# Seven products in one more tile, sums stored one after another, and separate PSUM banks at the end

## The chip, the cores and the metric

The kernel runs on one core of a Trainium2 chip. The metric is the device time of one execution in microseconds (us). The profile gives a second figure, the *span*, from the first to the last recorded event on the core; it is 1.7 to 3.2 us shorter than the device time. A profile also gives the mean granted clock of the matrix engine (1.00 is full speed).

Engines: PE multiplies matrices (PEld is its weight load, which overlaps), DVE is the vector engine, ACT the scalar engine, POOL the GpSimd engine, SP the engine that issues most stores. PSUM is the memory that PE writes its results into; it is divided into banks.

## The reference

Attention over 8 batches, 8 heads, 576 positions and head size 64, with a local mask for half of the heads and a strided one for the others, and then a gated product on the 4,608 tokens. Only the second part is touched:

```python
def _moe_ref(x, w_a, w_b, w_out):          # x: 4608 x 512
    a = x @ w_a                            # 512 x 1536
    b = x @ w_b
    return (a * b @ w_out).astype(np.float32)   # w_out: 1536 x 512
```

## The kernel before

The 4,608 tokens are 9 tiles of 512 (`TTOK`). For each tile the kernel makes 12 chunks (`FD`) of `pf = (x w_a) * (x w_b)`, 8 matmuls of 512 columns per chunk (the *projections*), and then the output `pf @ w_out`. The attention of later batches is woven between these matmuls. `do(slot, ...)` puts work after a given slot; there are 16 slots per tile, 12 for the projections and 4 for the output.

The output is computed in two ways. The ordinary way (`ffn_y`, in tiles 0 to 2) takes 48 matmuls of 512 columns. In the tiles of `FAST_Y` the rows, the contraction and the columns are each cut into two halves, and the four blocks of the output come from seven products of half size instead of eight. That takes 84 matmuls of 256 columns, but it needs sums of `pf` (`fast_s`, made by DVE for each tile, written into `ps`), sums of `w_out` (`fast_w`, made once, written into `wf`) and some additions and subtractions after the products.

```python
FAST_Y = (3, 4, 5, 6, 7, 8)
HT = TTOK // 2;  HN = d_model // 2;  FG = FD // 2

def fast_w(n, gs):                         # one of five sums of w_out, for the groups gs of 6
    a, b, op = (...)[n]
    nc.vector.tensor_tensor(wf[:, n, gs], a[:, gs], b[:, gs], op=op)

def fast_s(t, n, gs):                      # five sums of pf; group outermost: [group][sum, row]
    if t not in pss:
        pss[t] = nat.tile([128, 5 * FD * TTOK // 4], BF16, ...).rearrange("p (g m) -> p g m", g=FG)
    s = pss[t][:, gs]
    x = pfs[t].rearrange("p (g e) (i m) -> p g e i m", e=2, i=2)[:, gs]
    if n == 0:   tensor_tensor(s[:, :, 0:HT], x[:, :, 0, 0], x[:, :, 1, 1], op=ALU.add)
    elif n == 1: ...                       # sums 1 and 2 in one operation
    else:        ...                       # sums 3 and 4 in one operation

def products(t):                           # weights of a matmul: 128 neighbouring columns
    full = lambda e, i: (lambda g, q: pf[:, 2 * g + e, HT * i + 128 * q:HT * i + 128 * (q + 1)])
    summed = lambda n: (lambda g, q: s[:, g, HT * n + 128 * q:HT * n + 128 * (q + 1)])
    ...

def y_store(eng, t, y, i, q, n=...):       # 128 rows: 8 runs (a) of 16 rows (s)
    rows = out[...].rearrange("(q a i s) c -> a s i q c", q=2, i=2, s=16)
    eng.dma_start(out=rows[:, :, i, q], in_=y[i][:, q, n])
```

The last tile has its own form, `y_tail`, which runs the seven products once for each half `q` of the rows, to be done sooner:

```python
for q in range(2):
    if q == 0:
        bank = {x: mm_bank([128, HN]) for x in "abcd"}
    else:                                  # the last pass: two tiles of two banks each
        o = psum4["o"].tile([128, 2, 512], F32, tag="o", name="end")
        st = pst.tile([128, 2, 512], F32, tag="st", name="end")
        bank = {"a": o[:, 0, :HN], "b": o[:, 1, :HN], "c": st[:, 0, :HN], "d": st[:, 1, :HN]}
    for k in "3412567":
        ...                                # six matmuls, then ACT, DVE or POOL, then a store
```

The schedule of the parts that move: two fills of value buffers by POOL in slots 18 and 19 (tile 1), and ten pieces of the weights' sums by DVE in slots 33 to 42 (tile 2).

The softmax here doesn't subtract the row's maximum and nothing guards it: scores larger than these inputs give would overflow.

Of the kernel before, what the change touches and what calls it, by code (L numbers as in the profile page):

```python
# [7 lines left out]
F32 = mybir.dt.float32  # L8
BF16 = mybir.dt.bfloat16
# [17 lines left out]
FAST_Y = (3, 4, 5, 6, 7, 8)  # L27
# [3 lines left out]
def kernel(  # L31
# [10 lines left out]
    nc = tc.nc  # L42
# [122 lines left out]
    HT = TTOK // 2  # L165
    HN = d_model // 2
# [18 lines left out]
    def load_qk(b, strided, heads=range(HL), names="kq"):  # L185
        for nm in names:
            src = {"k": k, "q": q}[nm]
            if b < FIRST_D:
                n, R, h0 = (NP, RS, HL) if strided else (96, RL, 0)
                w0 = {"k6": 0, "q6": 1536, "k8": 3072, "q8": 5120}[f"{nm}{R}"]  # L190
                if b not in shared:
                    shared[b] = nat.tile([128, 5 * FD * TTOK // 4], BF16, tag="shared", name="shared")
# [304 lines left out]
    def step_X(b, c):  # L497
# [16 lines left out]
                 10.5: "V6", 11: "S0 Tk1", 11.5: "V7", 12: "Tq1 S1", 12.5: "V0 X2", 13: "S2", 13.5: "V1 X3 S3", 14: "V2",  # L514
# [5 lines left out]
    FN = {"Tk": step_Tk, "Tq": step_Tq, "S": step_S, "V": step_V, "X": step_X}  # L520
# [51 lines left out]
    def fast_s(t, n, gs):  # L572
        if t not in pss:
            pss[t] = nat.tile([128, 5 * FD * TTOK // 4], BF16, tag="shared", name="ps").rearrange("p (g m) -> p g m", g=FG)
        s = pss[t][:, gs]
        x = pfs[t].rearrange("p (g e) (i m) -> p g e i m", e=2, i=2)[:, gs]
        if n == 0:
            nc.vector.tensor_tensor(s[:, :, 0:HT], x[:, :, 0, 0], x[:, :, 1, 1], op=ALU.add)  # L578
        elif n == 1:
            nc.vector.tensor_tensor(s[:, :, HT:3 * HT].rearrange("p g (i m) -> p g i m", i=2), x[:, :, 0], x[:, :, 1], op=ALU.add)  # L580
        else:
            nc.vector.tensor_tensor(s[:, :, 3 * HT:].rearrange("p g (e m) -> p g e m", e=2), x[:, :, :, 1], x[:, :, :, 0],
                                    op=ALU.subtract)
# [3 lines left out]
    def products(t):  # L587
        pf, s = pfs[t], pss[t]
        full = lambda e, i: (lambda g, q: pf[:, 2 * g + e, HT * i + 128 * q:HT * i + 128 * (q + 1)])
        summed = lambda n: (lambda g, q: s[:, g, HT * n + 128 * q:HT * n + 128 * (q + 1)])  # L590
        wsum = lambda n: (lambda g: wf[:, n, g])
        wfull = lambda e, j: (lambda g: wov[:, e, j, g])
        return {"3": ("a", full(0, 0), wsum(0)), "4": ("b", full(1, 1), wsum(1)), "1": ("c", summed(0), wsum(2)),
                "2": ("b", summed(2), wfull(0, 0)), "5": ("a", summed(1), wfull(1, 1)), "6": ("c", summed(3), wsum(3)),
                "7": ("d", summed(4), wsum(4))}
# [7 lines left out]
    def y_store(eng, t, y, i, q, n=slice(0, d_model)):  # L603
        rows = out[TTOK * t:TTOK * (t + 1), n].rearrange("(q a i s) c -> a s i q c", q=2, i=2, s=16)
        eng.dma_start(out=rows[:, :, i, q], in_=y[i][:, q, n])
# [4 lines left out]
    def y_plan(t):  # L610
# [4 lines left out]
        def store_half(i):  # L615
            for q in range(2):
                y_store(nc.sync, t, y, i, q)
# [38 lines left out]
    def y_tail(t):  # L656
# [4 lines left out]
        for q in range(2):  # L661
            if q == 0:
                bank = {x: mm_bank([128, HN]) for x in "abcd"}
            else:
                o = psum4["o"].tile([128, 2, 512], F32, tag="o", name="end")
                st = pst.tile([128, 2, 512], F32, tag="st", name="end")
                bank = {"a": o[:, 0, :HN], "b": o[:, 1, :HN], "c": st[:, 0, :HN], "d": st[:, 1, :HN]}
# [74 lines left out]
    with tc.manual_schedule(engines={ENG.PE, ENG.SP, ENG.Pool, ENG.DVE, ENG.Activation}):  # L742
# [80 lines left out]
        def do(i, fn, *args):  # L823
            at.setdefault(i, []).append(lambda: fn(*args))
# [34 lines left out]
        do(18, fill_v, vl_buf[1])  # L859
        do(19, fill_v, vs_buf[1])  # L860
        for n in range(5):
            for z in range(2):
                do(33 + 2 * n + z, fast_w, n, slice(3 * z, 3 * z + 3))
# [48 lines left out]
```

## Time and profile before

| | |
|---|---|
| device time, median of 6 runs (the 3 given and 3 beside the changed kernel) | 337.37 us (336.41 to 339.04) |
| span of the profiled run | 335.3 us |
| tiles 0, 1, 2 | 41.19, 35.94, 35.21 us |
| tiles 3 to 7 | 34.23, 34.47, 34.22, 33.98, 29.89 us |
| projections of tile 8 | 20.72 us |
| its output, from the first product to the last DVE operation | 11.84 us |
| from that operation to the end of the span | 4.63 us |

A tile runs from its first projection to that of the next one. The prediction below shows the page, the chain and the waits. More views, two here and two behind the prediction:

The first is the timeline of the last pass of the last tile. Columns: start, length, engine, line, operation, out<-in, size, count, and in brackets the idle time before it and what ended that.

```profile
323.50 0.82 PE L678 MATMUL end<-wf,pf 128*128 128x256 bf16 x6
324.36 0.37 ACT L683 COPY ya<-end 128x256 f32<-128x256 f32 x1 [1.59 <-PE end L678]
...
324.78 0.82 PE L678 MATMUL end<-wf,pf 128*128 128x256 bf16 x6 [0.46 <-ACT ya L683]
...
327.46 0.81 PE L678 MATMUL end<-wo_sb,ps 128*128 128x256 bf16 x6 [0.46 <-ACT y_sb L693]
...
330.38 0.29 DVE L706 TENSOR_TENSOR y_sb<-ye,mm 128x128 f32<-128x128 f32 x1
```

PE stands still each time another engine reads the other half of the same two-bank tile. The last DVE operation ends at 330.67, 7.17 us after the pass began.

The second is DVE's timeline in tile 0, around the place where the change puts half of the weights' sums.

```profile
47.38 0.69 DVE L433 TENSOR_TENSOR xr<-o,rc 72x512 bf16<-72x512 f32 x1
51.54 0.46 DVE L374 TENSOR_TENSOR p<-p,mask_l 128x576 int16<-128x576 int16 x1 [3.47 <-ACT p L364]
```

DVE is idle for 3.47 us between these two.

The third is the busy time by stretch after the last DVE operation, when only stores are under way. Columns: stretch, length, busy PE, PEld, DVE, ACT, POOL with counts, clock, mean busy share of the 16 DMA engines, GB/s.

```profile
330.70:333.50 2.80, 0.00 (x0) 0.00 (x0) 0.00 (x0) 0.00 (x0) 0.00 (x0) 1.00 0.40 118
331.10:331.60 0.50, 0.00 (x0) 0.00 (x0) 0.00 (x0) 0.00 (x0) 0.00 (x0) 1.00 0.51 152
```

In no half microsecond after the last DVE operation is the share above 0.54: about eight of sixteen engines.

### The profile page before, as it was taken

The numbers are of one execution on the slowest core, as the hardware profiler recorded it, in microseconds if no ns is written. First come the engines' busy times: TensorE is split into PE (matmuls) and PEld (weight loads), VectorE is DVE, ScalarE is ACT, GpSimd is POOL, SyncE is SP. The second block draws the span as 40 slices with busy tenths as digits, with TensorE's granted clock in tenths as the row PEclk, the third lists the DMA queues.
The fourth block names the chain that finished last, engine by engine and source line by source line (L and its number), as shares of the span: only waits on it lengthen the run. The fifth ranks groups of instructions, "written<-read, shape, count | busy, mean of one in ns | idle before, by whom it ended". The sixth has DMA issues, their size and how long they took to land.

```text
span 335.3 us, 7662 instructions
## 1 busy us (share of the span) xinstructions
PE 326.2 (97%) x2814; PEld 201.8 (60%) x2814; DVE 254.7 (76%) x489; ACT 202.8 (60%) x329; POOL 173.4 (52%) x295
## 2 busy tenths in 40 slices
PE   8999999999999999999999999999999999999992
PEld 6654555455555555556999885568556844674472
DVE  5867566768878985799999999999877845738641
ACT  5663955468678865776587757875788533223320
POOL 8945836499956644765577457754312031312011
PEclk9999999999999999999999999999999999999999
DMA  9999999599999599969888998899123021003013
GB/s 155 148 203 196 201 181 188 120 191 70 131 221 155 86 99 158 129 116 92 69 83 139 179 98 75 142 164 107 25 62 119 2 73 54 1 12 116 0 29 98
DMA packets 102173, 37.60 MB, mean 112 GB/s; under 512 B 77432, under 2 KB 97784, under 8 KB 102136
## 3 DMA queue, kind: packets, MB, share of 16 engines
q0 software_dynamic: 87760, 19.58, 64.4%
q1 hardware_dynamic: 14104, 17.34, 17.7%
q8 instruction: 22, 0.36, 0.4%
q10 hardware_dynamic: 272, 0.20, 0.2%
q14 instruction: 15, 0.12, 0.1%
HBM read 39.71 MB, written 9.44 MB: 147 GB/s over the span
## 4 chain that ended last, share of the span: by engine, by line
PE 75%; DMA 12%; POOL 7%; DVE 2%; issue 2%; ACT 0%; DVEq 0%; POOLq 0%
PE mm L545 44%; PE mm L650 14%; PE mm L730 7%; DMA vl<-in_v_dram 4%; PE o L454 4%; PE st L356 3%; DMA shared<-in_k_dram 3%; DMA wa_sb<-in_moe_w_a_dram 3%; PE end L678 1%; PE mm L678 1%; POOL shared L195 1%; DMA kl<-in_k_dram 1%; POOL ql L210 1%; DMA natk<-in_k_dram 1%; POOL vl L222 1%
## 5 line engine op out<-in xcount | busy, mean ns | idle before, releaser
L545 PE MATMUL mm<-xT,wb_sb 128*128 128x512 bf16 (+1 forms) x472 | 110.2, 357 | 0.1
L545 PE MATMUL mm<-xT,wa_sb 128*128 128x512 bf16 (+1 forms) x472 | 110.3, 358 | 0.0
L562 ACT COPY a_sb<-mm 128x512 f32<-128x512 f32 x106 | 62.2, 587 | 48.7 <-PE mm L545 46.4
L545 PEld LDWEIGHTS <-wb_sb 128*128 128x128 bf16 x480 | 46.4, 98 | 44.5 <-issue 0.6
L880 POOL CAST pace<-pf 1x1 f32<-1x1 bf16 x84 | 28.4, 339 | 85.1 <-DVE pf L565 73.8
L565 DVE TENSOR_TENSOR pf<-a_sb,mm 128x512 bf16<-128x512 f32 x72 | 48.5, 674 | 17.2 <-PE mm L545 13.8
L545 PEld LDWEIGHTS <-wa_sb 128*128 128x128 bf16 x480 | 42.6, 98 | 31.2
L364 ACT ACTIVATE p<-st 128x576 bf16<-128x576 f32 (+1 forms) x64 | 41.7, 651 | 9.5 <-PE st L356 9.0
L463 ACT ACTIVATE xr<-o 64x576 f32<-64x576 f32 x48 | 31.1, 648 | 26.1 <-PE o L454 25.9
L730 PE MATMUL mm<-wo_sb,pf 128*128 128x512 bf16 x144 | 34.4, 379 | 0.5 <-DMA wo_sb<-in_moe_w_out_dram 0.5
L464 ACT ACTIVATE xr<-xr 64x576 f32<-64x576 f32 x48 | 32.9, 685 | 1.5
L650 PEld LDWEIGHTS <-ps 128*128 128x128 bf16 x300 | 28.5, 98 | 4.4 <-DVE ps L578 1.2
L567 DVE TENSOR_TENSOR pf<-a_sb,mm 128x512 bf16<-128x512 f32 x34 | 23.0, 678 | 8.4 <-ACT a_sb L562 5.9
L470 DVE TENSOR_TENSOR xT<-o,xr 64x288 bf16<-64x288 f32 x48 | 21.5, 448 | 10.4 <-ACT xr L464 9.7
L468 DVE TENSOR_TENSOR xT<-o,xr 64x288 bf16<-64x288 f32 x48 | 21.5, 447 | 8.9 <-ACT xr L464 8.3
L374 DVE TENSOR_TENSOR p<-p,mask_l 128x576 int16<-128x576 int16 x32 | 19.8, 618 | 6.8 <-ACT p L364 6.7
L650 PE MATMUL mm<-wf,ps 128*128 128x256 bf16 x180 | 22.7, 273 | 0.1
L234 POOL DMA_DIRECT2D vs<-in_v_dram x24 | 19.7, 821 | 4.1 <-PE st L356 2.8
L730 PEld LDWEIGHTS <-pf 128*128 128x128 bf16 x144 | 12.9, 98 | 13.9 <-issue 0.8
L880 POOL COPY pace<-y_sb 1x1 f32<-1x1 f32 x18 | 3.2, 177 | 34.0 <-ACT y_sb L633 14.8
L210 POOL DMA_DIRECT2D ql<-in_q_dram x24 | 16.0, 666 | 6.2 <-DMA wo_sb<-in_moe_w_out_dram 4.2
L210 POOL DMA_DIRECT2D kl<-in_k_dram x24 | 16.1, 671 | 4.0 <-issue 3.8
(155 smaller groups left out, 493.7 us busy)
## 6 DMA issues: line engine op xcount, KB each, us to landing
out_dram<-y_sb SPq DMA_DIRECT2D x34, 256.0 KB
vl<-in_v_dram POOLq DMA_DIRECT2D x7, 384.0 KB, 7.2
kl<-in_k_dram POOLq DMA_DIRECT2D x24, 72.0 KB, 3.1
ql<-in_q_dram POOLq DMA_DIRECT2D x24, 72.0 KB, 3.2
vs<-in_v_dram POOLq DMA_DIRECT2D x24, 72.0 KB, 3.8
wo_sb<-in_moe_w_out_dram POOLq DMA_DIRECT2D x4, 384.0 KB, 11.2
natk<-in_k_dram POOLq DMA_DIRECT2D x20, 72.0 KB, 3.2
natq<-in_q_dram POOLq DMA_DIRECT2D x20, 72.0 KB, 3.5
```

What stands on the lines that cost most here:

```text
L210: nc.gpsimd.dma_start(out=t[32 * h:32 * h + 32], in_=src[b, h].rearrange("(i y) d -> y i d", y=32))
L364: nc.scalar.activation(p[:M, :, :W], st[:M, :, :W], ACT.Exp, scale=scale)
L463: nc.scalar.activation(r, sums, ACT.Ln)
L464: nc.scalar.activation(r, r, ACT.Exp, scale=-1.0)
L468: nc.vector.tensor_mul(dst[:, W * half:W * (half + 1)], o[:64, j, :W], r[:, j])
L545: nc.tensor.matmul(ps_[:, c0:c0 + n], lhsT=w[:, kk, 128 * f:128 * (f + 1)], rhs=xT[:, kk, x0:x0 + n], start=(kk == first and c0 == 0), sto ...
L562: nc.scalar.copy(a_sb, ab[0])
L565: nc.vector.tensor_mul(pf[:, f, :].rearrange("p (i a s) -> p a i s", i=2, s=16), halves(a_sb), halves(ab[1]))
L567: nc.vector.tensor_mul(pf[:, f, :], a_sb, ab[1])
L650: nc.tensor.matmul(bank[b][:, q], lhsT=lhs(g, q), rhs=rhs(g), start=new and q == 0 and g == 0, stop=g == FG - 1, skip_group_check=True)
L730: nc.tensor.matmul(y, lhsT=pf[:, f, 128 * j:128 * (j + 1)], rhs=wo_sb[:, f], start=(f == 0), stop=(f == FD - 1))
L880: nc.gpsimd.tensor_copy(pace, done)
```

## The change

The intent: one more tile in the cheaper form; to make room on DVE in that tile, the weights' sums are made earlier, in tiles 0 and 1; each sum of `pf` lies in one piece, and the stores of tiles 2 to 7 write longer runs (those of the last tile keep their sizes); and the last pass gets PSUM banks that do not wait for each other.

```diff
-FAST_Y = (3, 4, 5, 6, 7, 8)
+FAST_Y = (2, 3, 4, 5, 6, 7, 8)
+    SW = HT + 16
@@ schedule of batch 1 (slot 11.5 is in tile 0): half of the weights' sums
-  11.5: "V7", ...
+  11.5: "V7 W0 W1 W2 W3 W4", ...
+  FN = {..., "W": lambda b, n: fast_w(n, slice(0, 3))}
@@ fast_s: sum outermost, group inside, 16 elements of gap
-   pss[t] = nat.tile([128, 5 * FD * TTOK // 4], ...).rearrange("p (g m) -> p g m", g=FG)
-   s = pss[t][:, gs]
+   pss[t] = nat.tile([128, FG * 5 * SW], ...).rearrange("p (n g m) -> p n g m", g=FG, n=5)
+   s = pss[t][:, :, gs, :HT]
-   nc.vector.tensor_tensor(s[:, :, 0:HT], x[:, :, 0, 0], x[:, :, 1, 1], op=ALU.add)
+   nc.vector.tensor_tensor(s[:, 0], x[:, 0, 0], x[:, 1, 1], op=ALU.add)
    ... (the other two likewise)
@@ products: even and odd rows
-   full = lambda e, i: (lambda g, q: pf[:, 2 * g + e, HT * i + 128 * q:HT * i + 128 * (q + 1)])
-   summed = lambda n: (lambda g, q: s[:, g, HT * n + 128 * q:HT * n + 128 * (q + 1)])
+   full = lambda e, i: (lambda g, q: pf[:, 2 * g + e, HT * i + q:HT * (i + 1):2])
+   summed = lambda n: (lambda g, q: s[:, n, g, q:HT:2])
@@ y_store and store_half
-   rows = out[...].rearrange("(q a i s) c -> a s i q c", q=2, i=2, s=16)
+   rows = out[...].rearrange("(a i s q) c -> a s i q c", i=2, s=8, q=2)
-   for q in range(2):
-       y_store(nc.sync, t, y, i, q)
+   rows = out[...].rearrange("(a i s q) c -> a s i (q c)", i=2, s=8, q=2)
+   nc.sync.dma_start(out=rows[:, :, i], in_=y[i].rearrange("p q c -> p (q c)"))
@@ y_tail, last pass
-   o = psum4["o"].tile([128, 2, 512], F32, tag="o", name="end")
-   st = pst.tile([128, 2, 512], F32, tag="st", name="end")
-   bank = {"a": o[:, 0, :HN], "b": o[:, 1, :HN], "c": st[:, 0, :HN], "d": st[:, 1, :HN]}
+   bank = {"a": psum4["o"].tile([128, 2, 512], F32, tag="o", name="end")[:, 0, :HN],
+           "b": pst.tile([128, 2, 512], F32, tag="st", name="end")[:, 0, :HN],
+           "c": mm_bank([128, HN]), "d": mm_bank([128, HN])}
@@ schedule
-   do(18, fill_v, vl_buf[1]);  do(19, fill_v, vs_buf[1])
-   for n in range(5):
-       for z in range(2):
-           do(33 + 2 * n + z, fast_w, n, slice(3 * z, 3 * z + 3))
+   do(27, fill_v, vl_buf[1]);  do(28, fill_v, vs_buf[1])
+   for n, slot in enumerate((16, 16, 19, 20, 22)):
+       do(slot, fast_w, n, slice(3, 6))
```

(The other user of the shared buffer, `shared`, only gets the new size.)

More of the change, by code (lines that the diff above doesn't have):

```diff
@@ L191, in load_qk @@
                 if b not in shared:
-                    shared[b] = nat.tile([128, 5 * FD * TTOK // 4], BF16, tag="shared", name="shared")
+                    shared[b] = nat.tile([128, FG * 5 * SW], BF16, tag="shared", name="shared")
                 t = nats[b, nm, strided] = shared[b][:n, w0:w0 + HL * R * D].rearrange("p (h r d) -> p h r d", r=R, d=D)
@@ L513 @@
     STEPS = {1: {5: "Tk2", 5.5: "Tk3", 6: "Tq2", 7: "S4", 7.5: "Tq3", 8: "S5", 8.5: "V4", 9: "S6 Tk0", 9.5: "V5", 10: "S7 Tq0",
-                 10.5: "V6", 11: "S0 Tk1", 11.5: "V7", 12: "Tq1 S1", 12.5: "V0 X2", 13: "S2", 13.5: "V1 X3 S3", 14: "V2",
+                 10.5: "V6", 11: "S0 Tk1", 11.5: "V7 W0 W1 W2 W3 W4", 12: "Tq1 S1", 12.5: "V0 X2", 13: "S2", 13.5: "V1 X3 S3", 14: "V2",
                  14.5: "V3 X0", 15: "X1"},
@@ L519 @@
              11: "V5", 12: "S7", 12.5: "V6", 14: "V7"}
-    FN = {"Tk": step_Tk, "Tq": step_Tq, "S": step_S, "V": step_V, "X": step_X}
+    FN = {"Tk": step_Tk, "Tq": step_Tq, "S": step_S, "V": step_V, "X": step_X, "W": lambda b, n: fast_w(n, slice(0, 3))}
     def run(b, slot):
@@ L573, in fast_s @@
         if t not in pss:
-            pss[t] = nat.tile([128, 5 * FD * TTOK // 4], BF16, tag="shared", name="ps").rearrange("p (g m) -> p g m", g=FG)
-        s = pss[t][:, gs]
-        x = pfs[t].rearrange("p (g e) (i m) -> p g e i m", e=2, i=2)[:, gs]
+            pss[t] = nat.tile([128, FG * 5 * SW], BF16, tag="shared", name="ps").rearrange("p (n g m) -> p n g m", g=FG, n=5)
+        s = pss[t][:, :, gs, :HT]
+        x = pfs[t].rearrange("p (g e) (i m) -> p e i g m", e=2, i=2)[:, :, :, gs]
         if n == 0:
-            nc.vector.tensor_tensor(s[:, :, 0:HT], x[:, :, 0, 0], x[:, :, 1, 1], op=ALU.add)
+            nc.vector.tensor_tensor(s[:, 0], x[:, 0, 0], x[:, 1, 1], op=ALU.add)
         elif n == 1:
-            nc.vector.tensor_tensor(s[:, :, HT:3 * HT].rearrange("p g (i m) -> p g i m", i=2), x[:, :, 0], x[:, :, 1], op=ALU.add)
+            nc.vector.tensor_tensor(s[:, 1:3], x[:, 0], x[:, 1], op=ALU.add)
         else:
-            nc.vector.tensor_tensor(s[:, :, 3 * HT:].rearrange("p g (e m) -> p g e m", e=2), x[:, :, :, 1], x[:, :, :, 0],
-                                    op=ALU.subtract)
+            nc.vector.tensor_tensor(s[:, 3:], x[:, :, 1], x[:, :, 0], op=ALU.subtract)
     yst = {}
@@ L603, in y_store @@
     def y_store(eng, t, y, i, q, n=slice(0, d_model)):
-        rows = out[TTOK * t:TTOK * (t + 1), n].rearrange("(q a i s) c -> a s i q c", q=2, i=2, s=16)
+        rows = out[TTOK * t:TTOK * (t + 1), n].rearrange("(a i s q) c -> a s i q c", i=2, s=8, q=2)
         eng.dma_start(out=rows[:, :, i, q], in_=y[i][:, q, n])
@@ L615, in store_half @@
         def store_half(i):
-            for q in range(2):
-                y_store(nc.sync, t, y, i, q)
+            rows = out[TTOK * t:TTOK * (t + 1)].rearrange("(a i s q) c -> a s i (q c)", i=2, s=8, q=2)
+            nc.sync.dma_start(out=rows[:, :, i], in_=y[i].rearrange("p q c -> p (q c)"))
         def post(k):
@@ L858 @@
         do(17, rezero, 1)
-        do(18, fill_v, vl_buf[1])
-        do(19, fill_v, vs_buf[1])
-        for n in range(5):
-            for z in range(2):
-                do(33 + 2 * n + z, fast_w, n, slice(3 * z, 3 * z + 3))
+        do(27, fill_v, vl_buf[1])
+        do(28, fill_v, vs_buf[1])
+        for n, slot in enumerate((16, 16, 19, 20, 22)):
+            do(slot, fast_w, n, slice(3, 6))
         for g in range(FG):
```

## The prediction

> **What bounds the kernel now.** I began with the page of the kernel before, first the busy times. PE, the matrix engine, is busy for all but 9 us of the span; DVE, the next, has 80 us to spare.
>
> ```profile
> PE 326.2 (97%) x2814; PEld 201.8 (60%) x2814; DVE 254.7 (76%) x489; ACT 202.8 (60%) x329; POOL 173.4 (52%) x295
> ```
>
> Busy is not yet bound, so the next view is the chain of work that ended last, in order of time. From 96 us to the end it is almost only PE, stage after stage. Columns: start, length, what.
>
> ```profile
> 124.49 3.89 PE mm L730 x18
> ...
> 268.38 20.72 PE mm L545 x96
> 289.10 9.17 PE mm L650 x84
> ```
>
> These lines give the rates. The first two projections (L545) take 20.72 us for 96 matmuls of 512 columns, 215.8 ns each; the ordinary output projection (L730) takes 3.89/18 = 216 ns; the seven-product form (L650) takes 9.17/84 = 109.2 ns for 256 columns. PE issues with no gap. Then the busy time by stretch, for tile 2 (96.11 to 131.32, ordinary output) and tile 3 (131.32 to 165.55, seven products); columns: stretch, length, busy PE, PEld, DVE, ACT, POOL, clock, DMA share, GB/s:
>
> ```profile
> 96.11:131.32 35.21, 35.21 (x260) 18.13 (x258) 29.02 (x57) 25.01 (x42) 19.71 (x37) 1.00 1.05 145
> 131.32:165.55 34.23, 34.20 (x297) 21.64 (x294) 30.81 (x57) 25.00 (x40) 19.98 (x37) 1.00 0.91 101
> ```
>
> PE fills both. Tile 3 does what tile 2 will do and is 0.98 us shorter. DMA is at 1.05 and 0.91 of its engines' time beside a full PE, so transfers are hidden there.
>
> The 9 us without PE lie at both ends: some 1 us before it starts, some stalls up to 60 us, 5 us after its last matmul, and three stalls in the last tile. The waits of PE list those three; columns: who waited for whom, total, times, longest.
>
> ```profile
> PE end L678 <- DVE y_sb L703: 0.6, 1, 0.6
> ...
> PE mm L730 <- DMA wo_sb<-in_moe_w_out_dram: 0.5, 1, 0.5
> PE end L678 <- ACT y_sb L693: 0.5, 1, 0.5
> PE end L678 <- ACT ya L683: 0.5, 1, 0.5
> ```
>
> In the chain the same place alternates between PE and the engine that empties PSUM:
>
> ```profile
> 323.67 0.67 PE end L678 x6
> 324.33 0.02 issue
> 324.36 0.38 ACT ya L683
> 324.74 0.04 issue
> 324.78 2.23 PE end L678 x18
> ```
>
> Here product 4, into half b of a two-bank tile, waits for ACT to read half a of the same tile. The data need no such order; sharing one tile makes it.
>
> **What the Trainium skill says.** (1) "TensorE: Matmul & The Clock Gate", Back-to-back issue gap, gives N/2.4 + 2.5 ns for a warm clock: 215.8 and 109.2 ns for 512 and 256 columns. The trace agrees to the digit. (2) The same page, Weight-path perf modes, says that a fast load of 128 weights reads four chunks of 32 columns, "packed or strided", with a column step of up to 1,024 elements. The change reads weights with a step of two. No load in the trace before is strided, so the trace is silent on that; it does show that a contiguous load has slack: eight 72-column matmuls, each with its own 128-column load, take 0.26 us, 33 ns each, against 109 ns per product. (3) "VectorE: DVE Perf Modes", the perf-mode tier table, gives tensor_tensor on bf16 in SBUF two elements per cycle; with its fixed 151 cycles, 1024 elements come to 691 ns. The trace has 680 to 693 ns for the sums of that size. (4) "SBUF — State Buffer", Who interferes with whom, says a DVE instruction with two SBUF inputs contends with a GpSimd one that reads SBUF. The trace agrees: at 166.82 us a mask operation took 1.97 us in place of 0.45, across a POOL subtraction of 1.28 us.
>
> **The change part by part.**
>
> Seven products in tile 2. Removed: 48 matmuls of 512 columns, 48 x 215.8 ns = 10.36 us. Added: 84 of 256, 9.17 us. Both lie on PE's path: minus 1.19 us. Against it: in tiles 3 to 6 PE waits for a late sum (waits of PEld: 1.2 us in four times, so 0.3 each, about 0.2 of it a gap on PE), and tile 2 will have that too. Net minus 1.0, which is also the 0.98 between the two tiles.
>
> DVE in tile 2 takes on sums of 5.0 us (L578 1.1, L580 1.9, L582 2.0 per tile) and four PSUM operations of 0.67 to 0.69 us, 2.7 together; it loses ten weight-sum operations of 0.533, 5.3 us. 29.0 + 7.7 - 5.3 = 31.4 us of 34.2: fuller than tile 3, under tile 5's 33.3 of 34, where PE does not stall. Time: none. ACT does three copies for four.
>
> Weights' sums in tiles 0 and 1. The five in tile 0 come to 5 x 0.533 = 2.7 us, right after DVE's work that ends at 48.07. DVE then idles 3.47 us, to 51.54. They fit in the hole, and the half of the output weights they read had arrived when PE used it at 45.4. The other five spread over tile 1, where DVE has 25.5 busy of 35. Its evictions may run a microsecond late, inside the slack of the PSUM buffers. Time: none, with a stall of some 0.3 us possible. The buffer fills, moved from slots 18 and 19 to 27 and 28, are POOL work off the path.
>
> Contiguous sums with a gap of 16 elements: the same number of DVE instructions over as many elements with unit step, so the same durations. Even and odd output rows: weight loads get step two, discussed above, and each half tile of output goes out as one DMA of 512 KB with runs of 4 KB, not two of 256 KB with 2 KB. Fewer packets, but DMA ends nothing in tiles 2 to 7. Time: none.
>
> PSUM banks of the last half pass. Products a and b now have a tile each, c and d come from the rotating banks, whose readers finished at about 322.8, before this pass starts at 323.5. Six matmuls are 0.655 us, but product 3 to 4 took 1.28 (323.50 to 324.78), 2 to 5 1.28 (326.18 to 327.46), and 6 to 7 1.40 (328.11 to 329.51): an excess of 0.62 + 0.62 + 0.75 = 2.0 us. Not all of it shows at the end. Product 5 would end at 3.28 us from the start of the pass; with the drain (0.17), the ACT copy and POOL's two subtractions of 0.73, the first waiting on product 2's copy, POOL ends at about 4.7, and the last two DVE operations at about 5.4. Before, they ended at 330.67 - 323.50 = 7.17. Gain 1.8 us, and POOL is the new limit of those last steps.
>
> **Sum:** 337.25 - 1.0 - 1.8 = 334.4 us.
>
> **The rivals.** (a) Strided weight loads are slow. If a load fell to one column per cycle at 1.2 GHz it would need 107 ns, just under the 109 of a matmul; if twice that, six tiles of 84 and the last one's 90 would each lose up to 100 ns, about 60 us. For it: no strided load has been seen here. Against it: a threefold slack, and point 2. (b) DVE becomes the bound, from tile 2 into tile 3: tile 2 leaves its last operations and two POOL subtractions to tile 3, with the contention of point 4. If the slack is used up, 1 to 2 us of PE stalls return and the time is about 336. Against it: tiles 4 to 6 already live like that. (c) The tail's stalls were hiding something else, the output queue: five stores take 7.7 us of issue from 323.6, and if the last one's issue and landing set the end, half of the 1.8 us stays, and the time is 335.3. (d) The larger output runs free DMA in the first 60 us, where PE does wait on it. No: no half-tile store changes there, so nothing.
>
> **Range and chances.** The mechanisms sum to a gain of 0.8%; 2% would be 6.7 us, more than all the stalls that the change touches. So faster by over 2% gets 0.03. Slower by over 2% needs rival (a), 0.04. The rest, 0.93, is within 2%. The runs before spread from 336.41 to 339.04, so the 8-in-10 range is 332.6 to 336.8, the upper side holding rivals (b) and (c).
>
> **What would show it.** Tile 2 should take 34.2 us, with 84 matmuls at 109 ns; spacing above 110 ns would be rival (a). In the last half pass the waits of PE for ACT and DVE should be gone and the pass end about 5.4 us after its start. DVE's hole at 48 to 51.5 us should hold five weight sums, with PE's waits up to 95 us no longer than before. Sums of 1024 elements should stay near 0.68 us. The prediction is wrong if new waits of PE for DVE add over 1 us in tiles 1 to 3, or if the strided loads show.

## More of the kernel before

The fourth is the DMA view from 322 us to the end.

```profile
DMA packets 954, 1.07 MB, mean 60 GB/s; under 512 B 56, under 2 KB 696, under 8 KB 952
```

There are 56 packets under 512 bytes. Seven stores end in this window, so that is 8 for each.

## The result

The changed kernel took 333.68 us, the median of 6 runs (332.72 to 336.13), against 337.37 for the kernel before (6 runs). The ratio of the fast runs is 0.9885, with a 95% interval of 0.9845 to 0.9926. Fast runs are those within 1.5% of the fastest run of the same kernel. Ratios here are the mean time of one kernel's fast runs over the mean of the other's from the same rounds, so they are not quite the ratio of the medians quoted. A second series (*after_again*) gave 332.89 us and 0.9871 [0.9826, 0.9917]. So the change is faster by 1.1 to 1.3%, the same within 2%; the prediction was 334.4, with a range of 332.6 to 336.8.

**One thing first: the head of the run.** The profiled run of the changed kernel was the slowest of its six, 336.13 us. Its page shows PE's busy time, and in the clock row one weak slice:

```profile
PE 324.0 (97%) x2818; PEld 206.3 (62%) x2850; DVE 264.3 (79%) x500; ACT 202.3 (61%) x328; POOL 175.8 (53%) x296
...
PEclk9959999999999999999999999999999999999999
...
out_dram<-y_sb SPq DMA_DIRECT2D x12, 512.0 KB, 5.0
```

The waits of PE name a transfer that came late (columns: who waited for whom, total us, times, longest):

```profile
PE o L411 <- DMA vl<-in_v_dram: 1.4, 1, 1.4
...
PE mm L678 <- DVE ps L581: 0.3, 1, 0.3
```

PE stood still for 1.36 us at 13.7 us, and the clock was 0.50 from 17.4 us to about 24 us. The first projection of tile 0 started at 21.80 us instead of 18.98. In *after_again* the head was good (18.92 us, clock 1.00). The kernel before has such runs too: one with a mean clock of 0.984 had a span of 340.1 us against 335.6. So such runs are not peculiar to the change. I therefore compare stages from tile 0 on, and spans of runs with a mean granted clock of at least 0.995, which I call *undisturbed*: the median is 335.6 us for the kernel before (30 of the 34 runs beside the three series of experiments), 331.25 for the changed one (6 of 7, the six and one run more), 330.9 in *after_again* (5 of 6). The gain in undisturbed spans is 4.35 us and 4.7 us.

| us, from one profile each | before | changed | *after_again* |
|---|---|---|---|
| first projection starts | 18.98 | 21.80 | 18.92 |
| tile 0 | 41.19 | 41.28 | 41.08 |
| tile 1 | 35.94 | 35.57 | 35.51 |
| tile 2 | 35.21 | 34.23 | 34.23 |
| tiles 3 to 7, sum | 156.79 | 156.80 | 156.78 |
| projections of tile 8 | 20.72 | 20.71 | 20.72 |
| its output, to the last DVE operation | 11.84 | 10.33 | 10.32 |
| from there to the end | 4.63 | 3.38 | 3.34 |

The busy time by stretch of the changed kernel, with the columns as above: tile 2, a piece of the disturbed head, and the stores at the end.

```profile
98.65:132.88 34.23, 33.99 (x293) 21.65 (x294) 30.93 (x57) 25.03 (x41) 20.02 (x37) 1.00 0.96 119
17.40:20.00 2.60, 2.60 (x48) 2.03 (x47) 1.33 (x3) 1.70 (x3) 0.67 (x1) 0.50 1.35 208
330.70:333.00 2.30, 0.00 (x0) 0.00 (x0) 0.01 (x1) 0.00 (x0) 0.00 (x0) 1.00 0.63 171
331.70:332.20 0.50, 0.00 (x0) 0.00 (x0) 0.00 (x0) 0.00 (x0) 0.00 (x0) 1.00 1.00 293
```

Tile 2 takes what tile 3 takes, and DVE has 30.93 us in it. The last two rows are the surprise: the stores now keep all sixteen DMA engines busy at their best, at 293 GB/s. In the kernel before, half a microsecond after the last DVE operation had a share of 0.54 and 180 GB/s at most.

DVE's hole in tile 0 of the changed kernel, in the timeline (the run is shifted by its late start):

```profile
51.67 2.42 DVE L175 TENSOR_TENSOR wf<-wo_sb 128x768 bf16<-128x768 bf16 x5
54.59 0.46 DVE L375 TENSOR_TENSOR p<-p,mask_l 128x576 int16<-128x576 int16 x1 [0.50 <-ACT p L365]
```

The five sums fit, and 0.50 us is left.

The last tile in its timeline, from product 2 of the first pass on:

```profile
322.79 1.48 PE L678 MATMUL mm<-wo_sb,ps 128*128 128x256 bf16 x12 [0.27 <-DVE ps L581]
...
325.42 1.47 PE L678 MATMUL end<-wf,pf 128*128 128x256 bf16 x12
...
328.79 1.49 PE L678 MATMUL mm<-wf,ps 128*128 128x256 bf16 x18
...
329.46 0.73 POOL L699 TENSOR_TENSOR ye<-ye,y_sb 128x256 f32<-128x256 f32 x1
...
330.23 0.49 DVE L706 TENSOR_TENSOR y_sb<-ye,mm 128x128 f32<-128x128 f32 x2
```

In the last pass PE goes through without a wait, and POOL's subtraction is what the last DVE operations follow; the pass ends 5.30 us after its start, at 330.72. But the first row has a wait that the kernel before did not have: product 2 waits 0.27 us for a sum.

The groups of the changed kernel, by shape (columns: line, engine, operation, out<-in with sizes, count, busy us, mean ns of one, idle before):

```profile
L583 DVE TENSOR_TENSOR ps<-pf 128x1024 bf16<-128x1024 bf16 x18 | 12.3, 681 | 0.0
...
L650 PEld LDWEIGHTS <-ps 128*128 128x128 bf16 x360 | 34.2, 98 | 5.3 <-DVE ps L579 1.5
```

A contiguous sum takes 681 ns (680 before), and a load of every second column 98 ns, as a packed one did before.

### The profile page after: what moved, and what is told of

It is laid out like the page before. It is cut to its first block, busy times and chain, and to the rows that moved or that the text cites. A ratio compares the mean times of both kernels' runs of the same rounds, so it can differ in the third digit from the quotient of the medians.

```text
span 334.1 us, 7692 instructions
## 1 busy us (share of the span) xinstructions
PE 324.0 (97%) x2818; PEld 206.3 (62%) x2850; DVE 264.3 (79%) x500; ACT 202.3 (61%) x328; POOL 175.8 (53%) x296
## 4 chain that ended last, share of the span: by engine, by line
PE 80%; DMA 12%; POOL 4%; issue 1%; DVE 1%; POOLq 0%; ACT 0%; DVEq 0%
PE mm L546 49%; PE mm L650 17%; DMA vl<-in_v_dram 4%; PE mm L730 4%; PE o L455 4%; PE st L357 4%; DMA shared<-in_k_dram 3%; DMA wa_sb<-in_moe_w_a_dram 3%; PE mm L678 1%; DMA natk<-in_k_dram 1%; POOL shared L196 1%; POOL vl L223 1%; PE end L678 1%; POOL wa_sb L244 0%; DVE tk L300 0%
## 5 line engine op out<-in xcount | busy, mean ns | idle before, releaser
L546 PE MATMUL mm<-xT,wa_sb 128*128 128x512 bf16 (+1 forms) x452 | 108.8, 357 | 0.9
L546 PE MATMUL mm<-xT,wb_sb 128*128 128x512 bf16 (+1 forms) x464 | 108.8, 357 | 0.3
L879 POOL CAST pace<-pf 1x1 f32<-1x1 bf16 x84 | 29.2, 347 | 83.2 <-DVE pf L566 80.8
L566 DVE TENSOR_TENSOR pf<-a_sb,mm 128x512 bf16<-128x512 f32 x84 | 56.4, 671 | 17.0 <-PE mm L546 13.7
L546 PEld LDWEIGHTS <-wa_sb 128*128 128x128 bf16 x480 | 42.7, 98 | 31.4 <-issue 0.3
L650 PEld LDWEIGHTS <-ps 128*128 128x128 bf16 x360 | 34.2, 98 | 5.3 <-DVE ps L579 1.5
L650 PE MATMUL mm<-wf,ps 128*128 128x256 bf16 x216 | 27.3, 273 | 0.2
L375 DVE TENSOR_TENSOR p<-p,mask_l 128x576 int16<-128x576 int16 x32 | 22.3, 696 | 2.6 <-ACT p L365 2.6
L730 PE MATMUL mm<-wo_sb,pf 128*128 128x512 bf16 x93 | 22.6, 379 | 0.2
L650 PE MATMUL mm<-wf,pf 128*128 128x256 bf16 x144 | 17.6, 273 | 0.0
```

Of the source, the lines that this page charges most:

```text
L375: nc.vector.tensor_tensor(pi, pi, mk, op=ALU.bitwise_and)
L546: nc.tensor.matmul(ps_[:, c0:c0 + n], lhsT=w[:, kk, 128 * f:128 * (f + 1)], rhs=xT[:, kk, x0:x0 + n], start=(kk == first and c0 == 0), sto ...
L566: nc.vector.tensor_mul(pf[:, f, :].rearrange("p (i a s) -> p a i s", i=2, s=16), halves(a_sb), halves(ab[1]))
L650: nc.tensor.matmul(bank[b][:, q], lhsT=lhs(g, q), rhs=rhs(g), start=new and q == 0 and g == 0, stop=g == FG - 1, skip_group_check=True)
L730: nc.tensor.matmul(y, lhsT=pf[:, f, 128 * j:128 * (j + 1)], rhs=wo_sb[:, f], start=(f == 0), stop=(f == FD - 1))
L879: nc.gpsimd.tensor_copy(pace, done)
```

## The experiments

**Theory**: the gain is the sum of independent parts. Tile 2 gives 1.0 us, the banks give up to 1.9, and the row layout speeds up the stores at the end, because they are spread over 16 DMA engines in place of 8. **Rivals**: the layout's longer runs and fewer packets make the stores faster, not the engines; DVE or the strided loads take something back; the moves of the weights' sums are not needed. Each kernel is a version of the one before or of the changed one; the diff says of which. By the ratios of the fast runs alone, e1, e2, e4, e6 and e8 cannot be told from the kernel before (their intervals include 1); what each part does is therefore read from the stages, and undisturbed spans are given beside them.

### e1: the banks alone, in the kernel before

```diff
-   bank = {"a": o[:, 0, :HN], "b": o[:, 1, :HN], "c": st[:, 0, :HN], "d": st[:, 1, :HN]}
+   bank = {"a": (own "o" tile), "b": (own "st" tile), "c": mm_bank([128, HN]), "d": mm_bank([128, HN])}
```

> The kernel before with only the new PSUM banks of the last half pass. Theory (the shared two-bank tile orders PE behind ACT and DVE): the three waits of PE in that pass vanish, the pass from its first product to the last DVE operation falls from 7.2 to about 5.4 us, all tile lengths stay, and the time falls by 1.8 us (ratio 0.9945). Rival (the output queue sets the end): the pass is shorter but the end moves by under 1 us.

Measured: 336.34 us, ratio 0.9986 [0.9945, 1.0026]; undisturbed span 334.4, a gain of 1.15 us. (The kernel before has 335.55 in the series of e1 to e4.) The output of tile 8 took 9.95 us to the last DVE operation in place of 11.84, so the banks remove 1.89 us there. But from that operation to the end it took 5.27 us, not 4.63. The stretches after the last DVE operations show why:

```profile
328.80:332.20 3.40, 0.00 (x0) 0.00 (x0) 0.04 (x1) 0.00 (x0) 0.00 (x0) 0.83 0.46 141
329.30:329.80 0.50, 0.00 (x0) 0.00 (x0) 0.00 (x0) 0.00 (x0) 0.00 (x0) 1.00 0.47 107
```

The results are ready sooner, and the stores then take longer at about half of the engines: the last data packet comes 3.19 us after the last DVE operation, where it was 2.55. With the old layout the transfers set the end, and part of the gain is lost to them.

### e2: the layout alone

Sums with the sum outermost, even and odd rows, and the new stores, in the kernel before; nothing else.

```diff
-   s = pss[t][:, gs]
+   s = pss[t][:, :, gs, :HT]            (as in the change, with products, y_store and store_half)
```

> The kernel before with only the contiguous sums, the weight loads of step two with even and odd output rows, and the merged stores. Theory (loads and stores are hidden): tiles 3 to 7 keep 34.23, 34.47, 34.22, 33.98 and 29.89 us to 0.05, 84 products at 109.2 ns, stores 12 fewer of twice the size, time within 0.3 us of before, but 0.3 us may be lost in the last tile, where product 2 waited for a sum in the changed kernel's profile and not before. Rival (loads of step two are slower): output passes longer than 9.17 us.

Measured: 336.35 us, ratio 0.9985 [0.9955, 1.0014]; undisturbed span 334.35, a gain of 1.2 us, more than the 0.3 that the theory allowed. From the last DVE operation to the end it is 2.98 us in place of 4.63. Against that, the output of the last tile took 12.19 us in place of 11.84, with the new wait of 0.3 us for a sum in it. Tile 1 took 37.15 us in this profile, more than in the kernel before; the changes of e2 do not touch tile 1, and I come back to that under e10. The weight loads took 98 ns, as before, and the sums what they take in the changed kernel (618, 679 and 692 ns for the same shapes, within 1 ns).

### e3: tile 2 and its moves alone

```diff
-FAST_Y = (3, 4, 5, 6, 7, 8)
+FAST_Y = (2, 3, 4, 5, 6, 7, 8)           (and the weights' sums and the fills in their new slots)
```

> The kernel before with only the seven-product form in tile 2 and the moved weight sums and fills. Theory (PE bound, minus 10.36 plus 9.17 plus a wait of 0.2): tile 2 falls from 35.21 to 34.2 us, tile 1 from 35.9 to 35.6 as in the changed kernel, tile 0 stays, the time falls by 1.0 to 1.4 us (ratio 0.996). Rival (DVE becomes the bound): waits of PE for DVE in tiles 1 to 3 grow by over 1 us and the time does not fall.

Measured: 335.34 us, ratio 0.9943 [0.9917, 0.9969]; undisturbed span 333.6, a gain of 1.95 us. Tile 2 took 34.23 us (minus 0.98), as in the changed kernel:

```profile
95.12:129.35 34.23, 34.20 (x297) 21.65 (x295) 30.94 (x57) 25.02 (x41) 20.05 (x37) 1.00 0.97 124
```

Tile 1 took 35.51 us (minus 0.43) and tile 0 40.65. (Tile 0 lies anywhere from 40.33 to 41.73 us in the fourteen profiles, without relation to the edits.) Tile 4 took 0.26 us more than in the kernel before; why is open. The end is as before: 11.84 and 4.66. The parts e1, e2 and e3 add up to 1.15 + 1.2 + 1.95 = 4.3 us of undisturbed span, against 4.35 and 4.7 for the changed kernel. So the parts add, as far as these medians can tell: undisturbed runs of one kernel lie up to 4.3 us apart.

### e4: the changed kernel without the moves

All of the weights' sums in tile 2, and the fills in slots 18 and 19, as before.

```diff
-   11.5: "V7 W0 W1 W2 W3 W4"             +   11.5: "V7"
-   do(27, fill_v, ...); do(28, fill_v, ...)   +   do(18, ...); do(19, ...)
-   for n, slot in enumerate((16, 16, 19, 20, 22)): do(slot, fast_w, n, slice(3, 6))
+   for n in range(5):
+       for z in range(2): do(33 + 2 * n + z, fast_w, n, slice(3 * z, 3 * z + 3))
```

> The changed kernel, but with the weight sums and the fills back where they were, in tiles 2 and 1. DVE then has 31.4 plus 5.3, some 36.7 us of work in a tile of 34.2. Theory (the move made room for tile 2): PE waits for DVE in tile 2 by 2 us or more, the tile is 36 us or longer, and the kernel is 1.5 to 3 us slower than the changed one (ratio to before about 0.995). Rival (DVE has slack enough and the move was needless): tile 2 stays at 34.2 us and the ratio is 0.989.

Measured: 336.89 us, ratio to the kernel before 1.000 [0.9971, 1.003]; undisturbed span 334.8. The stretch of tile 2:

```profile
96.58:133.56 36.98, 34.92 (x296) 21.33 (x294) 35.18 (x67) 25.01 (x41) 21.72 (x37) 1.00 0.89 114
```

And PE's waits:

```profile
PE mm L650 <- DVE pf L566: 1.4, 2, 0.8
```

DVE has 35.18 us of work, more than the 34.23 that PE needs. It is the bound of tile 2, which takes 36.98 us, 2.75 more than in the changed kernel. Without the moves the seventh tile would have cost time. It is the sums that cost it: e10, with only the fills put back, has 34.23 us in tile 2. Tile 1 took 36.85, 1.3 us more than in the changed kernel.

### e5: weights with a step of eight

In tiles 2 to 7 the products read their weights from `pf` with every eighth column; the sums are still made but not read. The result is wrong.

```diff
+   full = lambda e, i: (lambda g, q: pf[:, TTOK * g + HT * i + q:TTOK * g + HT * i + 8 * 128:8])
```

> Wrong result on purpose: the changed kernel, but the products of tiles 2 to 7 take their weights from the activations with a column step of 8 elements (16 bytes) in place of 2; the sums are still made but not read. Theory (a load has some threefold slack against a 109 ns matmul): even if a load takes twice as long it stays hidden, 84 products at 109.2 ns. Rival (wide steps are slow): the step-2 load was near its limit and at step 8 the spacing of products rises above 120 ns, the output passes become over 10 us long.

Measured: 332.38 us in one run (span 330.4, clock 1.00), the span of the changed kernel in a good run less 0.5. One group of the weight loads:

```profile
L660 PEld LDWEIGHTS <-pf 128*128 128x128 bf16 x504 | 54.9, 145 | 0.2
```

With a step of eight a load takes 145 ns, not 98: wider steps do cost. Yet the seven products of tile 7 still took 9.17 us, 109.2 ns each, so loads hide behind the products even so. (145 ns is more than the distance of two products, so the recorded times of neighbouring loads overlap: the 504 loads cover 54.9 us together, 109 ns each.) With a step of two there is nothing to hide: 98 ns.

### e6: the seven products in tile 1 too

```diff
-FAST_Y = (2, 3, 4, 5, 6, 7, 8)
+FAST_Y = (1, 2, 3, 4, 5, 6, 7, 8)
```

> The changed kernel with the seven-product form in tile 1 too. DVE had 25.5 us of 35 in tile 1 before, plus 2.7 of weight sums, plus 7.7: 35.9 of 34.4. Theory (DVE is nearly full there): PE waits for DVE in tiles 1 and 2 and gains 0 to 0.5 us over the changed kernel. Rival (PE bound as in tile 2): tile 1 falls from 35.6 to 34.6 us and the ratio to before is 0.986.

Measured: 336.01 us, ratio to the kernel before 0.9969 [0.9936, 1.0003]; undisturbed span 333.4, 2.1 to 2.5 us above the changed kernel. Neither the theory nor the rival expected a loss. Tile 1 took 38.21 us in place of 35.5:

```profile
59.71:97.92 38.21, 35.15 (x298) 21.40 (x300) 33.27 (x62) 24.73 (x41) 32.53 (x51) 1.00 1.15 123
```

Its waits of PE:

```profile
PE o L455 <- DVE xT L471: 1.8, 3, 0.9
PE mm L650 <- DVE pf L566: 1.0, 1, 1.0
```

Both lie in tile 1, and their 2.8 us are nearly all of the 3.06 us that PE is idle there. So PE waits for DVE. DVE has 33.27 us of work in a tile that would need about 34, and POOL 32.53. The sum alone does not explain it: in the kernel before, tiles 4 and 5 have 33.40 and 33.51 us of DVE work in 34.47 and 34.22, and PE does not stall. In those tiles POOL has 21 to 23 us of work. Whether POOL's load or the order of the work makes DVE late in tile 1 was not tested. This is what rival (b) of the prediction feared for tile 2. It did not come true there, because the moves took the load off, but it does in the next tile up.

### e8: banks and layout, without tile 2

```diff
 FAST_Y = (3, 4, 5, 6, 7, 8)              (with the edits of e1 and of e2)
```

> The kernel before with the layout and the banks, without tile 2 and the moves. Alone, the layout ended 3.0 us after the last DVE operation and the banks 5.3, before 4.6. Theory (the two parts need each other: the banks bring the last stores closer together, the even and odd rows store them faster): last DVE operation 1.6 us earlier than before, end 3.0 to 3.4 us after it, together a gain of 2.8 us (ratio 0.9915), more than 1.2 and 0.2 added. Rival (the parts add): 1.4 us, ratio 0.996.

Measured: 335.06 us, ratio 0.9958 [0.9915, 1.0001]; undisturbed span 332.8 (4 of 6 runs), a gain of 2.8 us. The sum of e1 and e2 is 2.35. If the layout frees what the banks lost to the stores in e1 (5.27 us at the end there, 3.26 here), the two together gain more than their sum. The difference has the right sign, but 0.45 us is too near the scatter of these medians to count as shown. The stages of the profiles say about the same: with the old layout the banks gain 1.89 us in the pass and lose 0.64 at the end, with the new one (e2 to e8) they gain 1.87 and lose 0.28.

### e9: banks, and stores over 16 engines without the rest of the layout

The store's runs are 8 rows in place of 16, and `pf` is split to match. Rows are not even and odd, the sums lie as before, the stores have the size and the runs of before; but the outermost dimension of the store's address pattern is 16 in place of 8.

```diff
-   halves = lambda x: x.rearrange("p (a i s) -> p a i s", i=2, s=16)
+   halves = lambda x: x.rearrange("p (a i s) -> p a i s", i=2, s=8)
-   rows = out[...].rearrange("(q a i s) c -> a s i q c", q=2, i=2, s=16)
+   rows = out[...].rearrange("(q a i s) c -> a s i q c", q=2, i=2, s=8)      (and the banks of e1)
```

> The banks-only kernel, with nothing else of the change but the split of tokens into halves by runs of 8 rows in place of 16: weights stay contiguous, there are no even and odd rows, and the slowest dimension of every output store is 16 in place of 8. Theory (a store is spread over as many DMA engines as divide its slowest dimension, 8 before and 16 after the change): the stores of the last passes carry 8 completion packets more each, the end comes 3.3 us after the last DVE operation in place of 5.3, and the time falls by 3 us against before (ratio 0.991). Rival (it is the even and odd rows' addresses that store faster): the end stays at 4.6 to 5.3 us after the last DVE operation and the ratio is that of the banks alone, 0.9966 in its undisturbed runs.

Measured: 334.80 us, ratio 0.9898 [0.9855, 0.9942]; undisturbed span 332.6 (4 of 6), 1.8 us less than e1. By the two profiles, 1.1 us of that lies after the last DVE operation (4.16 in place of 5.27), and the rest in tiles 0 and 1, which this edit does not touch. The stretch of the last stores:

```profile
329.30:329.80 0.50, 0.00 (x0) 0.00 (x0) 0.00 (x0) 0.00 (x0) 0.00 (x0) 1.00 1.00 287
```

The share of the DMA engines is 1.00 in place of 0.47, at 287 GB/s in place of 107, in the same stretch as in e1. Two numbers of one pattern did it. (They also change which rows lie side by side; the full share and the small packets below speak for the engines.) The DMA view from 322 us on, with the same line in the changed kernel:

```profile
DMA packets 1009, 1.06 MB, mean 59 GB/s; under 512 B 112, under 2 KB 752, under 8 KB 1008
```

It counts 112 packets under 512 bytes, twice the 56 of before: 16 for each of the seven stores, not 8. The larger packets are as many as before (640 from 512 bytes to 2 KB, 256 from there to 8 KB), in e9 and in the changed kernel. So the rival of longer runs and fewer packets is dead: the last tile has neither. The Trainium skill ("DMA: Bandwidth & Descriptors", Why a DMA increments its semaphore by 16 and not by 1) says how many engines a transfer gets: the largest number up to 16 that divides the slowest dimension of both address patterns, and each engine that takes part ends with its own small write. The traces agree: the slowest dimension is 8 before and 16 after, and the small packets double.

What the number of engines does not explain: from the last DVE operation to the end it took 4.16 us, not 3.3 as with the new layout. The traces divide this time at the last data packet. It comes 2.04 us after the last DVE operation in e9, 3.19 in e1, and 2.00 and 1.98 in the two profiles of the changed kernel: this part, 1.15 us, e9 has in full. After it only the program's closing instructions run (waits for semaphores, drains, a clearing of semaphores). They take 2.03 to 2.09 us in the four profiles with the old layout (the kernel before, e1, e3, e9) and 1.26 to 1.52 in the ten with the new one. Between e9 and *after_again* the difference is 0.69 us. SP passes its last waits one after another, about 0.06 us each. In both it passes one of them 0.36 us after the last packet; six more follow in e9 and two in *after_again*: 0.25 us. The rest, 0.43 us, lies between the clearing of the semaphores and the end of POOL's next drain (0.52 us and 0.09). Why that is longer is open.

### e10 and e12: the fills back in their old slots

```diff
-   do(27, fill_v, vl_buf[1]);  do(28, fill_v, vs_buf[1])
+   do(18, fill_v, vl_buf[1]);  do(19, fill_v, vs_buf[1])      (in the changed kernel; e12 is e10 again)
```

> The changed kernel with the two buffer fills of POOL back at slots 18 and 19. Theory (the fills hold up POOL's loads of the next batch, so DVE and then PE wait in tile 1): tile 1 rises from 35.6 us to 36 or more, with DVE waiting 1 us or longer for the transposed q blocks, and the ratio to before rises to 0.990 or more. Rival (tile 1 is shorter because of the weight sums in its slots, or by chance): tile 1 stays at 35.6 us.

> A second look at the changed kernel with the fills of POOL back at slots 18 and 19: its first profile had tile 1 at 39.7 us, yet three of its six runs were as fast as the changed kernel. If the fills cost time in every run, tile 1 is 36 us or longer here too; if they only make a bad run possible, tile 1 is 35.5 us.

Measured: e10 333.98 us, ratio 0.9908 [0.987, 0.9947]; its undisturbed spans are 331.2, 331.3, 331.4, 332.5 and 335.5 us. e12, one look, 334.53 us (span 332.5). In e10's profiled run, its slowest, tile 1 took 39.69 us, and 36.95 in e12. The waits of DVE in e10:

```profile
DVE tk L305 <- DMA natk<-in_k_dram: 3.2, 1, 3.2
```

and in e12:

```profile
DVE tk L305 <- DMA qz11l<-tq: 2.2, 1, 2.2
```

In tile 1 DVE waits for transfers that POOL has a hand in: with the fills early (e10), POOL issued the first of these loads 21.95 us after the tile's start, against 19.06 us with the fills late. The two fills, 1.41 and 1.82 us long, stand before it. So the fills can delay transfers that tile 1 waits for. But three runs of e10 are as fast as the changed kernel. What the late fills seem to buy is fewer bad runs of tile 1: in the profiles it is 0.2 to 4.2 us longer with early fills. Tile 1 of the kernels with the early fills took 35.94, 36.13, 37.15, 36.85, 36.44, 35.75, 39.69 and 36.95 us in their profiles; of the correct kernels with late fills and no seven products in tile 1, always 35.51 or 35.57. What decides between the runs with early fills is open.

### e11: mend the new wait

The sums now lie one after another. One DVE operation writes sums 1 and 2 together for one group, so the stretch of memory from its first to its last element holds all groups of one of them, and a product that reads only other groups waits for it. This version splits that operation in the last tile, sum 2 first, and makes sum 0 earlier in the other tiles.

```diff
-   fast_s(t, 1, slice(FG - 1, FG))
+   for i in (1, 0):
+       last_s(t, i)                       # one half of that operation each
-   ..., (10, 2, 2, 4), (11, 0, 2, 6), (11, 2, 4, 6), (12, 1, 2, 6)
+   ..., (10, 0, 2, 5), (11, 0, 5, 6), (11, 2, 2, 6), (12, 1, 2, 6)
```

> The changed kernel with the first-needed sum of each tile mostly made one slot earlier, and the last tile's last sum for products 5 and 2 made in two operations, that of product 2 first. Theory (each of tiles 2 to 6 loses about 0.2 us of PE to a late sum, the last tile 0.3 to a sum that its product need not wait for as a whole): those waits vanish, tiles 2, 3 and 5 fall from 34.23 to 34.0, tile 4 from 34.47 to 34.25, the last tile by 0.3; in all 1.2 us less than the changed kernel (ratio to before 0.985). Rival (DVE is as full as before and the wait moves to a later sum or to the projections' evictions): tiles unchanged, 0.3 us gained at most.

Measured: 332.18 us, ratio to the kernel before 0.9864 [0.9812, 0.9916]. On the same chip the changed kernel (*after_again*) took 332.89. Medians of the undisturbed runs are 331.83 and 332.86. The wait of product 2 in the last tile is gone: the output of tile 8 took 9.96 us, not 10.32, just the 9.95 of e1, where the sums lay as before. That the wait goes when the operation is split supports the explanation, and so does its place in the changed kernel: it stands before the first of product 2's matmuls, which reads another group. The wait in the other tiles did not go; it moved to the next sum:

```profile
PEld L655 <- DVE ps L581: 1.0, 4, 0.3
```

(1.5 us in five times in the changed kernel.) Tiles 2 to 5 gained 0.05 us each, tile 6 0.2. This is the fastest version I have, by about 1 us; the intervals of the two overlap.

### after_again: the changed kernel once more

> The changed kernel again, as a control on the same chip: ratio 0.9885, tiles 2 to 6 as before, last DVE operation 3.4 us before the end.

No edit. 332.89 us, ratio 0.9871 [0.9826, 0.9917]; its profile had a good head, and its stages are in the table above. The differences of its stages to the kernel before sum to the difference of the two spans, 330.9 minus 335.3 = minus 4.4, with nothing left over: minus 0.06 at the start, minus 0.11, 0.43 and 0.98 in tiles 0 to 2, minus 1.52 in the output of tile 8, minus 1.29 from there to the end, and 0.01 elsewhere.

## Why the prediction was right

Its time, 334.4 us, was 0.7 above the measured 333.68, inside the range, and the class was the one it gave 0.93. Step by step:

- **PE bounds the kernel.** Right. Tiles 3 to 7 did not move (156.79 and 156.78 us), and every part that gained either took work from PE, took a wait from it, or lay behind its last matmul.
- **Tile 2, minus 1.0.** Right: minus 0.98 in the changed kernel and in e3. The fifth wait for a sum came too (five times, 0.3 us each).
- **DVE in tile 2, 31.4 us, no time.** Right: 30.93. e4 shows that it was near: at 35.18 us DVE is the bound.
- **The hole of tile 0.** Right: the five sums took 2.42 us (2.7 predicted), and 0.50 us was left.
- **Tile 1, "Time: none".** Too low by 0.43 us on the good side. The fills were called "POOL work off the path"; e10 and e12 show that they can delay loads that DVE waits for.
- **Contiguous sums, the same durations.** The durations were right to 3 ns (681 in place of 680 for 1024 elements), but for one sum of 512 elements that runs beside a POOL subtraction in the last tile, before and after (1.49 and 1.62 us, the others 0.42). What the step missed is a wait: 0.27 us in the last tile (e2 has it, e1, e3 and e9 do not, e11 removes it).
- **Strided loads.** Right, and rival (a) is dead: 98 ns, products at 109.2 ns. e5 shows that a step of eight would lengthen the recorded load by 47 ns and still be hidden. (The 107 ns of the rival is from no trace of this case.)
- **Stores: "Time: none".** This is the term that was mis-sized. The argument was that DMA ends nothing in tiles 2 to 7. That is true, but the stores of the last tile end the kernel, and the step did not look there. From the last DVE operation to the end it is 1.25 to 1.3 us less: 4.63 to 3.38 and 3.34 (1.65 with the layout alone, and nearly 2 against the banks alone). Two things are in it. The last data packet comes 0.55 us sooner (2.55 to 2.00 and 1.98), and 1.2 us sooner than with the banks alone. The cause is not the fewer packets and longer runs that the prediction named, for the last tile has neither, but the number of DMA engines, which e9 tests alone. The other 0.7 us are the closing instructions after that packet, of which e9 explains only a part.
- **Banks, minus 1.8; the pass ends 5.4 us after its start.** Right: 5.30 in place of 7.17, minus 1.87, and POOL's subtraction is the new limit of the last steps. In the kernel before, it would not have been worth that: e1 gained 1.15 us, nearer to rival (c) than to 1.8, because the stores take over. With the new layout, to which the prediction gave nothing, more of the 1.9 us comes out: 1.59 by the profiles of e2 and e8, 1.25 by those of the kernel before and e1.
- **Rival (b), DVE as the bound.** Not in tile 2, but true in tile 1 (e6) and without the moves (e4). **Rival (d)** predicted nothing, and no transfer in the first 60 us changed for it.
- **Two readings.** DVE's busy time in tile 5 is 33.51 us of 34.22, not 33.3 of 34, and in tile 1 25.32 of 35.94, not 25.5 of 35. Neither changes a step. The sums called "of that size" in point 3 are those of 1024 elements.

The sum: predicted minus 1.0 and minus 1.8. Measured in undisturbed spans minus 0.98 and minus 1.87, then the three terms that were left out: after the last DVE operation minus 1.3, tile 1 minus 0.4, the new wait plus 0.3. With minus 0.2 in tile 0 and at the start, which is within their scatter, it is minus 4.4 in all. So the two terms of the sum were right, but that the time was met to 0.7 us is in part luck: the gain in undisturbed spans was about 1.6 times the 2.8 us predicted. By device time it was less, 3.7 by the medians. Part of this is the disturbed runs in both series. Part is that device time minus span is about 2.0 us in the kernels with the new layout and about 1.7 in the others, so some 0.3 us of the gain in span is given back outside of it; why is open.

## What to carry to other kernels

When a stage ends the kernel, read what comes after its last compute instruction as well: the share of the DMA engines in the last stores showed half of them idle, and one number in the store's address pattern (16 in place of 8 in its outermost dimension) brought the last packet 1.15 us sooner (e1 to e9), more than a tile's seven products gave (1.0). Read the closing instructions apart from the transfers: here they were 0.7 of the 1.3 us gained at the end. Before giving an engine more work in a stage, add up its busy time there against the bound: 31 of 34 us was free here, 33 was free in tiles 4 and 5 but not in tile 1, and 35 in tile 2 was not. Where an instruction writes two pieces that lie apart, expect readers of what lies between them to wait for it too.

## What the Trainium skill lacked or had wrong

- "DMA: Bandwidth & Descriptors", Why a DMA increments its semaphore by 16 and not by 1: its rule for the number of engines held (8 to 16, with 8 more small packets for each store), but that passage does not say what the number is worth at the end of a kernel (the page has a rate per engine elsewhere). Here the last stores ran at a share of 0.38 to 0.54 and 102 to 188 GB/s with a slowest dimension of 8, and at up to 1.00 and 287 to 293 GB/s with 16; the last packet came 1.15 us sooner for it (e1 to e9).
- "TensorE: Matmul & The Clock Gate", Back-to-back issue gap: its formula for an isolated matmul fits the sustained rate here, but its sustained figure of about 131 ns for 512 columns does not: 96 matmuls, each with its own weight load, took 20.72 us, 215.8 ns each. (The page's Part 1 has 215.7 ns for matmuls back to back, which agrees.)
- The same page, Weight-path perf modes: "packed or strided" holds for a step of two (98 ns both), but the page has no cost for wider steps, and the note on 16-byte lines in "SBUF — State Buffer" has none for a weight load either. Every eighth bf16 column (16 bytes) took 145 ns per recorded load.
- The same page, What's actually happening, has half clock after an idle window of about 3.4 us; its section on a second failure mode tells of frequent short stops with that effect, but gives no length. Here one stop of 1.36 us at 13.7 us, with smaller ones around it, was followed by a clock of 0.50 from 17.4 to about 24 us, and runs with a mean clock of 0.98 to 0.99 are 2 to 7 us longer, in every kernel that had some. Whether the stops alone cause it, no run here shows.
